# Attention and MoE on one core: the sign bit of a decoded weight from a multiplication by zero on GpSimd instead of a mask on VectorE

## The chip, the cores and the metric

The kernel runs on 1 core of one Trainium2 chip. The metric is the device time of one execution in microseconds (us). In the rows below PE is TensorE (PEld its weight loads), DVE is VectorE, ACT is ScalarE, POOL is GpSimd and SP is SyncE, which issues the DMAs.

## What is computed

The reference is attention that keeps the 32 best scores of each row, followed by four matrix products:

```python
scores = (q @ k.transpose(0, 1, 3, 2)) / sqrt(64)      # batch 8, heads 8, 576 x 576, head size 64
kth = np.partition(scores, -32, axis=-1)[..., -32:-31]
scores = np.where(scores >= kth, scores, -1e9)
attn = exp(scores - max); attn = attn / (sum(attn) + 1e-9)
x = (attn @ v) laid out as 4608 tokens x 512
out = (((x @ w1) * (x @ w2)) @ w3) @ w_out             # 512 -> 1024 -> 1024 -> 512
```

q, k and v are float32, the weights float64: each weight reaches the chip as a pair of 32-bit words, a low word and a high word, and the kernel turns the pair into a float32 by itself.

## The kernel before

**Attention slots.** The work is cut into 144 slots (8 batches, 18 slots each; a slot is 128 queries of two heads). The loop of line 504 runs over `p` and is software-pipelined: in turn `p` VectorE looks for the 32 best of slot `p` (`top32_steps`), GpSimd and ScalarE mask and exponentiate slot `p-1` (`edges_of`, `mask`, `exps`), TensorE computes the scores of slot `p+1`, and slot `p-2` is transposed, multiplied with V and normalised. Below "slot n" means turn `p = n` of this loop, counted from the moment VectorE starts the four min/max operations at its head (`w<-s` twice, `w<-w,s` twice), which I call the opening. `mask` may only start after the opening of the same turn (line 509).

**MoE blocks.** Every 12 slots give 384 tokens; their matrix products (`moe_steps`) are put in between the slots by `fill`, 24 matmuls a turn. The first block needs slots 0 to 11 through to their normalisation, so it starts in turn 14.

**Weights at the start.** 80 units of 128 x 256 weights (16 of `w_out`, 32 of `w3` mixed with 16 of `w1`, then 16 of `w2`) are fetched and decoded in turns 0 to 13. `warm` (line 487) is called six times a turn; each call takes one new unit and moves every unit on the way by one step, oldest first. For a unit taken in call k the steps are:

- call k: ScalarE writes `t`, the high word scaled by 2^-112, into PSUM, and `r`, the upper 16 bits of the low word scaled by 2^-13, as an integer into SBUF (lines 115, 116). Two units share a PSUM tile for `t`.
- call k+1: VectorE cuts the sign bit out of `t` (line 119, the **sign cut**), then shifts `t` left by 3 and ors the sign in (line 120, the **shift-or**), giving `u`.
- call k+2: GpSimd adds `u` and `r` as integers (line 123, the **integer add**).
- call k+4 and later: a `w3` unit is multiplied with `w_out` on TensorE (`pf`), because `w3 @ w_out` is folded into one matrix; every fourth one ends with a cast to `wf` on ScalarE and a subtraction on VectorE. A `w1` or `w2` unit is cast to `wh` on ScalarE and, one call later, its rest `wl` is computed by GpSimd (`wl<-z,wh`).

All engines run what they are given in program order (`InOrder`, line 47), so an instruction that waits holds up everything behind it on its engine. In the trace every operation carries the line of that helper, L57; rows are told apart by their tiles.

The line of the change reads, before:

```python
sign, u, r = (z[:, i * 256 : (i + 1) * 256].bitcast(I32) for i in range(3))
...
dve.tensor_scalar(sign, ti, -(2**31), None, op0=ALU.bitwise_and)
dve.scalar_tensor_tensor(u, ti, 3, sign, op0=ALU.logical_shift_left, op1=ALU.bitwise_or)
```

`z` has 768 words; the pairs fill 0 to 511. So `sign` and `u` were written over the pairs once ScalarE had read them, and `r` behind them.

Of the kernel before, what the change touches and what calls it, by code (L numbers as in the profile page):

```python
# [11 lines left out]
I32 = mybir.dt.int32  # L12
U16 = mybir.dt.uint16
AF = mybir.ActivationFunctionType
ALU = mybir.AluOpType
# [52 lines left out]
def attn_moe(ctx: ExitStack, tc: tile.TileContext, q, k, v, w1, w2, w3, w_out, out, flag, general):  # L68
    nc = tc.nc
    pe, act, dve, pool, sp = nc.tensor, nc.scalar, nc.vector, nc.gpsimd, nc.sync  # L70
# [26 lines left out]
    if not general:  # L97
        pe, act, dve, pool, sp = (InOrder(tc, e) for e in (pe, act, dve, pool, sp))
# [8 lines left out]
    def decode(z, dst=None):  # L107
        if not bank:
            both = ps_m.tile([128, 512], F32, tag="mm", name="t")
            bank.extend((both[:, 256:], both[:, :256]))  # L110
        t = bank.pop()
        high = z[:, 1:512:2]
        low = z[:, :512].bitcast(U16)[:, 1:1024:4]
        sign, u, r = (z[:, i * 256 : (i + 1) * 256].bitcast(I32) for i in range(3))
        act.activation(t, high, AF.Copy, scale=2.0**-112)
        act.activation(r, low, AF.Copy, scale=2.0**-13)
        yield
        ti = t.bitcast(I32)
        dve.tensor_scalar(sign, ti, -(2**31), None, op0=ALU.bitwise_and)
        dve.scalar_tensor_tensor(u, ti, 3, sign, op0=ALU.logical_shift_left, op1=ALU.bitwise_or)  # L120
        yield
        dst = z[:, :256] if dst is None else dst
        pool.tensor_tensor(dst.bitcast(I32), u, r, op=ALU.add)
        yield
        yield
        return dst

    def load_w12(i, c, z):
        if len(wl) == i:
            wl.append(const.tile([128, NCC * DF], F32R, tag="wl1", name="wl1"))  # L130
        cut = slice(c * 256, (c + 1) * 256)
        y = yield from decode(z)
        act.copy(wh[i][:, cut], y)
        yield
        pool.tensor_tensor(wl[i][:, cut], y, wh[i][:, cut].bitcast(F32), op=ALU.subtract)

    def load_wout(c, z):
        yield from decode(z, wo[:, c * 256 : (c + 1) * 256])
# [3 lines left out]
    def load_w3(c, z):  # L142
        f, i = c // 4, c % 4
        y = yield from decode(z)
        if i == 0:
            fold[f] = ps_m.tile([128, 512], F32, tag="mm", name=f"pf{f}")
        for j in range(2 * i, 2 * i + 2):
            pe.matmul(
                fold[f], y[:, (j % 2) * 128 : (j % 2 + 1) * 128], wo[:, j * DM : (j + 1) * DM],
                start=(j == 0), stop=(j == NFC - 1),  # L150
            )
        if i == 3:
            cut = slice(f * DM, (f + 1) * DM)
            yield
            act.copy(wf[0][:, cut], fold[f])
            yield
            dve.tensor_tensor(wf[1][:, cut], fold[f], wf[0][:, cut].bitcast(F32), op=ALU.subtract)
# [273 lines left out]
    for n in range(n_blocks):  # L431
        mine = sorted({group_of[i] for i in range(n * BLOCK, (n + 1) * BLOCK)}, key=lambda g: groups[g])
        lo, pieces = 0, []
        for g in mine:
            b, t = groups[g]
# [68 lines left out]
    for p in range(-1, n_slots + 3):  # L504
        i, j, m = p + 1, p - 1, p - 2
# [29 lines left out]
        if i < n_slots:  # L535
            b, hps, t = slots[i]
# [10 lines left out]
        if 0 <= m < n_slots:  # L547
            b, hps, t = slots[m]
# [86 lines left out]
```

## Time and profile before

| | |
|---|---|
| median of 3 runs | 1319.36 us (1319.17 to 1322.74) |
| the profiled execution | 1321.85 us, span 1320.0 us |
| TensorE busy | 1235.3 us, 94% of the span |
| VectorE busy | 1194.1 us, 90% |
| ScalarE busy | 965.9 us, 73% |
| GpSimd busy | 853.7 us, 65% |
| weights decoded | from 7.2 us (first `t`) to 207.0 us (last `wl`) |

How to read it: the profiled execution lies 2.49 us above the median, and its span 1.85 us below its own time. The shares are averages over two very different stretches, turns 0 to 13 with the decoding and the turns after them, so a view by stretch is needed.

### The profile page before, as it was taken

The page shows a single profiled execution, that of the slowest core. Times are in us where ns is not written, and L with a number is a line of the kernel's source. Part 1 is how long each engine was busy: PE and PEld are TensorE (multiplying, and loading weights), DVE is VectorE, ACT ScalarE, POOL GpSimd, SP SyncE. Part 2 cuts the span into 40 slices and gives each one's busy share as a digit, 9 for nine tenths or more (in the row PEclk, how much of TensorE's full clock was granted, in tenths as well). Part 3 has the DMA queues.
Part 4 walks back from the last instruction along what each step waited for, and adds up shares of the span by engine and source line. Part 5 has one row for each costly group of instructions (what it writes and reads, how often), then busy time and mean ns, then how long its engine had stood idle before and what let it go on. Part 6 is the DMA issues. An engine that isn't in the chain of part 4 may idle for free.

```text
span 1320.0 us, 28196 instructions
## 1 busy us (share of the span) xinstructions
PE 1235.3 (94%) x9617; PEld 1047.7 (79%) x9617; DVE 1194.1 (90%) x4012; ACT 965.9 (73%) x2057; POOL 853.7 (65%) x1225
## 2 busy tenths in 40 slices
PE   2788858999999999999999999999999999999996
PEld 1334436888888888888888888888888888888996
DVE  7988898999999999999999999999999999999610
ACT  5766786877777877777877877778777778777621
POOL 4767697666766766667757757757667666667510
PEclk9899967999999999999999999999999999999998
DMA  6333331200121001100120012110220012000000
GB/s 243 91 101 123 110 96 29 81 22 21 29 74 32 9 27 64 53 27 16 39 84 20 10 33 79 32 33 10 65 60 9 15 47 81 22 21 1 13 13 27
DMA packets 35886, 64.82 MB, mean 49 GB/s; under 512 B 6036, under 2 KB 12180, under 8 KB 35732
## 3 DMA queue, kind: packets, MB, share of 16 engines
q1 hardware_dynamic: 35732, 62.93, 15.3%
q8 instruction: 77, 1.26, 0.4%
q14 instruction: 77, 0.63, 0.2%
HBM read 53.48 MB, written 9.44 MB: 48 GB/s over the span
## 4 chain that ended last, share of the span: by engine, by line
PE 87%; DVE 4%; POOL 3%; ACT 2%; issue 2%; DMA 1%; SPq 0%; POOLq 0%
PE ab L57 32%; PE eo L57 16%; PE ro L57 15%; PE st L57 12%; PE tp L57 9%; PE pf L57 3%; DVE z L57 2%; DVE w L57 1%; POOL z L57 1%; DVE top L57 1%; POOL wl L57 1%; ACT pab L57 1%; DMA vt<-in_v 0%; ACT s L57 0%; ACT z L57 0%
## 5 line engine op out<-in xcount | busy, mean ns | idle before, releaser
L57 POOL TENSOR_TENSOR pab<-s,pab 128x576 f32<-128x576 f32 x288 | 404.2, 1426 | 127.5 <-DVE w L57 102.0
L57 DVE MAX8 top<-w 128x8 f32<-128x192 f32 (+1 forms) x1152 | 467.3, 447 | 0.0
L57 PE MATMUL ab<-x,wh 128*128 128x384 f32 x1536 | 403.7, 344 | 0.0
L57 ACT COPY pts<-tp 128x1024 f32<-128x1024 f32 x144 | 146.1, 1014 | 198.2 <-PE tp L57 196.8
L57 DVE MATCH_REPLACE8 w<-top,w 128x192 f32<-128x192 f32 x864 | 289.4, 343 | 0.0
L57 PEld LDWEIGHTS ab<-x,wh 128*128 128x128 f32 x1536 | 275.3, 189 | 0.0
L57 PE MATMUL ab<-x,wl 128*128 128x384 f32 x768 | 269.5, 351 | 0.0
L57 ACT ACTIVATE pab<-pab,edge 128x576 f32<-128x576 f32 x288 | 226.8, 787 | 0.5 <-POOL pab L57 0.5
L57 PE MATMUL eo<-g,wf 128*128 128x384 f32 x1152 | 225.8, 346 | 0.0
L57 ACT ACTIVATE pab<-s,edge 128x576 f32<-128x576 f32 x288 | 207.6, 768 | 7.6 <-POOL edge L57 7.5
L57 PE MATMUL st<-kt,qt 64*128 64x288 f32 (+1 forms) x1280 | 188.7, 443 | 18.4 <-ACT pts L57 7.4
L57 PEld LDWEIGHTS eo<-g,wf 128*128 128x128 f32 x1152 | 198.6, 188 | 7.5 <-issue 7.5
L57 ACT COPY s<-st 128x576 f32<-128x576 f32 x288 | 184.4, 640 | 19.5 <-PE st L57 19.5
L57 DVE TENSOR_TENSOR w<-w,s 128x384 f32<-128x384 f32 x288 | 183.9, 639 | 4.9
L57 DVE TENSOR_TENSOR w<-s 128x384 f32<-128x384 f32 x288 | 173.0, 642 | 7.4 <-ACT s L57 7.4
L57 PEld LDWEIGHTS ro<-pts,vt 128*64 128x64 f32 x2560 | 130.2, 139 | 51.3 <-ACT g L57 28.3
L57 PEld LDWEIGHTS st<-kt,qt 64*128 64x128 f32 (+1 forms) x1280 | 100.6, 183 | 81.0 <-ACT pr L57 28.1
L57 PE MATMUL ro<-pts,vt 128*64 128x128 f32 (+1 forms) x2560 | 163.4, 271 | 0.0
L57 PE MATMUL tp<-ident,pab 128*128 128x128 f32 x1152 | 152.1, 275 | 11.3 <-ACT s L57 11.3
L57 PEld LDWEIGHTS ab<-x,wl 128*128 128x128 f32 x768 | 144.3, 188 | 13.4 <-issue 12.3
L57 PEld LDWEIGHTS tp<-ident,pab 128*128 128x128 f32 x1152 | 136.4, 142 | 22.3 <-POOL wo L57 10.7
L57 POOL TENSOR_TENSOR g<-asb,g 128x384 fp32r<-128x384 f32 x96 | 96.9, 1010 | 86.8 <-ACT g L57 86.8
(51 smaller groups left out, 1309.6 us busy)
## 6 DMA issues: line engine op xcount, KB each, us to landing
z<-in_w SPq DMA_DIRECT2D x64, 256.0 KB, 2.7
vt<-in_v SPq DMA_DIRECT2D x32, 352.0 KB, 3.7
qt<-in_q SPq DMA_DIRECT2D x40, 256.0 KB, 2.7
kt<-in_k SPq DMA_DIRECT2D x32, 320.0 KB, 3.1
out_t<-osb SPq DMA_DIRECT2D x32, 192.0 KB, 1.9
z<-in_wo SPq DMA_DIRECT2D x16, 256.0 KB, 3.9
out_t<-osb SPq DMA_DIRECT2D x16, 160.0 KB, 1.8
out_t<-osb SPq DMA_DIRECT2D x16, 32.0 KB, 1.6
```

Of the source, the lines that this page charges most:

```text
L57: ins = fn(*args, **kw)
```

## The change

The sign bit is no longer cut out of `t` by VectorE. GpSimd multiplies the high words by 0.0, which leaves a zero with the sign of the weight, and writes it to words 512 to 767 of the tile (I call it the **zero product**). The shift-or takes it from there and writes `u` over it. `r` now goes into the low words of the pairs, with a stride of two words, and the integer add writes its sum over `u` unless the unit is one of `w_out`.

```diff
-        sign, u, r = (z[:, i * 256 : (i + 1) * 256].bitcast(I32) for i in range(3))
+        r, u = z[:, 0:512:2].bitcast(I32), z[:, 512:768].bitcast(I32)
         act.activation(t, high, AF.Copy, scale=2.0**-112)
+        pool.tensor_scalar(z[:, 512:768], high, 0.0, None, op0=ALU.mult)
         act.activation(r, low, AF.Copy, scale=2.0**-13)
         yield
-        ti = t.bitcast(I32)
-        dve.tensor_scalar(sign, ti, -(2**31), None, op0=ALU.bitwise_and)
-        dve.scalar_tensor_tensor(u, ti, 3, sign, op0=ALU.logical_shift_left, op1=ALU.bitwise_or)
+        dve.scalar_tensor_tensor(u, t.bitcast(I32), 3, u, op0=ALU.logical_shift_left, op1=ALU.bitwise_or)
         yield
-        dst = z[:, :256] if dst is None else dst
+        dst = z[:, 512:768] if dst is None else dst
         pool.tensor_tensor(dst.bitcast(I32), u, r, op=ALU.add)
```

GpSimd's order in a turn with `w3` and `w1` units, from `sums` (head of the turn) on. `edge`, `over`, `x` and `wide` belong to the attention, `pab` is the attention masking, `z<-z` as TENSOR_TENSOR the integer add. Before:

```order
L57 TENSOR_SCALAR sums<-sums 128x2
L57 TENSOR_TENSOR z<-z 128x256
L57 TENSOR_TENSOR edge<-top_96,coef 128x4
L57 TENSOR_TENSOR over<-top_96 128x2
L57 TENSOR_TENSOR x<-pr,x 128x128
L57 COPY wide<-sums 128x128
L57 TENSOR_TENSOR pab<-s,pab 128x576 x2
L57 TENSOR_TENSOR wl_103<-z,wh_98 128x256
L57 TENSOR_TENSOR z<-z 128x256
L57 TENSOR_TENSOR wl_103<-z,wh_98 128x256
L57 TENSOR_TENSOR z<-z 128x256 x4
```

The same stretch in the changed kernel (`TENSOR_SCALAR z<-z` is the zero product):

```order
L57 TENSOR_SCALAR sums<-sums 128x2
L57 TENSOR_TENSOR z<-z 128x256
L57 TENSOR_SCALAR z<-z 128x256
L57 TENSOR_TENSOR edge<-top_96,coef 128x4
L57 TENSOR_TENSOR over<-top_96 128x2
L57 TENSOR_TENSOR x<-pr,x 128x128
L57 COPY wide<-sums 128x128
L57 TENSOR_TENSOR pab<-s,pab 128x576 x2
L57 TENSOR_TENSOR wl_103<-z,wh_98 128x256
L57 TENSOR_TENSOR z<-z 128x256
L57 TENSOR_SCALAR z<-z 128x256
L57 TENSOR_TENSOR wl_103<-z,wh_98 128x256
```

One zero product stands ahead of `edge`, the other five of the turn stand behind the masking, each behind the integer add of its call and ahead of the next call's work.

VectorE's order in such a turn with what each row waits for, from the `wf` subtraction on. Before:

```order
L57 TENSOR_TENSOR wf_101<-pf_734,wf_100 128x512 [waits Activation_49]
L57 TENSOR_SCALAR z<-t 128x256 [waits DMAHW7_49,Activation_49]
L57 SCALAR_TENSOR_TENSOR z<-t,z 128x256 [waits DVE_49]
L57 MAX top_95<-w 128x8 x2
L57 MATCH_REPLACE w<-top_95,w 128x192 [waits DVE_49] x2
L57 TENSOR_SCALAR z<-t 128x256 [waits DMAHW0_49,Activation_49]
```

In the changed kernel:

```order
L57 TENSOR_TENSOR wf_101<-pf_868,wf_100 128x512 [waits Activation_49]
L57 SCALAR_TENSOR_TENSOR z<-t,z 128x256 [waits DMAHW4_49,Activation_49,Pool_49]
L57 MAX top_96<-w 128x8 x2
L57 MATCH_REPLACE w<-top_96,w 128x192 [waits DVE_49] x2
L57 SCALAR_TENSOR_TENSOR z<-t,z 128x256 [waits DMAHW6_49,Activation_49,Pool_49]
```

The sign cuts are gone, and the shift-or now waits for GpSimd as well.

## Rows read from the trace of the kernel before

**Rows 1.** The first part of the page: busy time, share of the span and instructions of each engine.

```profile
PE 1235.3 (94%) x9617; PEld 1047.7 (79%) x9617; DVE 1194.1 (90%) x4012; ACT 965.9 (73%) x2057; POOL 853.7 (65%) x1225
```

**Rows 2.** Busy time by stretch, one stretch a turn: slots 0, 1, 2, then 5 and 6, then 11, 12, 13, and last the time from slot 14 to 1290 us. Columns: stretch, its length, then busy us (and instructions) of PE, PEld, DVE, ACT and POOL, the granted TensorE clock, the DMA engines' busy share, GB/s.

```profile
7.38:18.19 10.81, 4.58 (x16) 2.45 (x16) 10.60 (x35) 4.49 (x12) 2.91 (x4) 1.00 1.04 390
18.19:30.54 12.35, 2.15 (x9) 1.78 (x9) 12.04 (x38) 8.24 (x20) 8.37 (x11) 1.00 0.46 131
30.54:43.39 12.85, 7.15 (x38) 4.36 (x38) 12.33 (x40) 9.73 (x23) 8.66 (x12) 1.00 0.46 146
...
72.87:89.07 16.20, 12.97 (x56) 6.23 (x55) 13.30 (x41) 10.81 (x26) 10.71 (x15) 0.89 0.35 99
89.07:103.64 14.57, 11.33 (x56) 5.75 (x55) 13.31 (x42) 10.83 (x26) 10.74 (x15) 1.00 0.42 127
...
165.15:179.63 14.48, 9.49 (x52) 6.03 (x50) 13.29 (x41) 12.25 (x31) 12.82 (x19) 0.76 0.41 110
179.63:194.09 14.46, 7.84 (x38) 4.88 (x38) 13.27 (x40) 11.52 (x30) 13.53 (x20) 0.54 0.37 109
194.09:206.35 12.26, 6.67 (x38) 4.29 (x38) 10.81 (x34) 9.24 (x23) 12.11 (x18) 0.56 0.01 1
206.35:1290.00 1083.65, 1080.68 (x8896) 957.27 (x8897) 1014.72 (x3479) 820.07 (x1707) 709.18 (x1016) 1.00 0.12 36
```

**Rows 3.** VectorE's groups by shape, the two of the decoding: count, then busy us and mean ns of one, then idle time before them and what ended it.

```profile
L57 DVE SCALAR_TENSOR_TENSOR z<-t,z 128x256 int32<-128x256 int32 x80 | 34.0, 424 | 2.7
L57 DVE TENSOR_SCALAR z<-t 128x256 int32<-128x256 int32 x80 | 33.3, 417 | 8.1 <-ACT z L57 7.6 <-issue 0.4
```

**Rows 4.** VectorE in order of time in slot 1: start us, duration us. Two units follow each other here without anything between them.

```profile
20.72 0.42 DVE L57 TENSOR_SCALAR z<-t 128x256 int32<-128x256 int32 x1
21.17 0.42 DVE L57 SCALAR_TENSOR_TENSOR z<-t,z 128x256 int32<-128x256 int32 x1
21.51 0.41 DVE L57 TENSOR_SCALAR z<-t 128x256 int32<-128x256 int32 x1
```

**Rows 5.** GpSimd's groups by shape that bear on the price of the zero product (columns as in rows 3).

```profile
L57 POOL TENSOR_SCALAR sums<-sums 128x2 f32<-128x2 f32 x144 | 30.9, 214 | 119.6 <-ACT pab L57 118.6 <-DVE top L57 0.5
L57 POOL TENSOR_TENSOR wl<-z,wh 128x256 fp32r<-128x256 f32 x32 | 23.3, 729 | 1.3 <-ACT wh L57 1.0
...
L89 POOL MEMSET over<- 128x288 f32 x1 | 0.3, 338 | 0.0
...
masks.py:197 POOL MEMSET ident<- 128x128 f32 x1 | 0.2, 205 | 0.3 <-POOLq L618 0.3
```

**Rows 6.** Order of time in slot 1: the integer add at the turn's head, the masking, and the third shift-or of the turn.

```profile
18.41 0.92 POOL L57 TENSOR_TENSOR wo<-z 128x256 int32<-128x256 int32 x1 [1.38 <-issue]
...
20.95 2.77 POOL L57 TENSOR_TENSOR pab<-s,pab 128x576 f32<-128x576 f32 x2 [0.68 <-DVE w L57]
...
23.92 0.42 DVE L57 SCALAR_TENSOR_TENSOR z<-t,z 128x256 int32<-128x256 int32 x1
```

**Rows 7.** Order of time in slot 6, all engines (start us, duration us; in brackets the idle time of the engine before it and what ended it).

```profile
90.93 0.59 ACT L57 CAST wf<-pf 128x512 fp32r<-128x512 f32 x1 [1.03 <-PE pf L57]
...
92.37 1.43 ACT L57 ACTIVATE pab<-s,edge 128x576 f32<-128x576 f32 x2
...
93.22 2.78 POOL L57 TENSOR_TENSOR pab<-s,pab 128x576 f32<-128x576 f32 x2 [1.10 <-ACT pab L57]
...
95.97 0.72 POOL L57 TENSOR_TENSOR wl<-z,wh 128x256 fp32r<-128x256 f32 x1
...
96.65 0.72 POOL L57 TENSOR_TENSOR z<-z 128x256 int32<-128x256 int32 x1
...
97.42 1.98 PE L57 MATMUL pf<-wo,z 128*128 128x512 f32 x4 [2.63 <-POOL z L57]
...
98.00 0.42 DVE L57 SCALAR_TENSOR_TENSOR z<-t,z 128x256 int32<-128x256 int32 x1
...
99.34 1.24 PE L57 MATMUL st<-kt,qt 64*128 64x288 f32 x8
...
100.14 0.64 ACT L57 COPY s<-st 128x576 f32<-128x576 f32 x1 [0.92 <-PE st L57]
...
100.51 1.09 PE L57 MATMUL ro<-pts,vt 128*64 128x128 f32 x16
...
101.75 2.41 PE L57 MATMUL pf<-wo,z 128*128 128x512 f32 x5
101.94 0.29 DVE L57 TENSOR_TENSOR pr<-ro,pr 128x128 f32<-128x128 f32 x1 [0.22 <-POOL sums L57]
...
102.77 0.42 DVE L57 TENSOR_SCALAR z<-t 128x256 int32<-128x256 int32 x1 [0.54 <-ACT z L57]
...
103.64 0.54 DVE L57 TENSOR_TENSOR w<-s 128x384 f32<-128x384 f32 x1
```

**Rows 8.** GpSimd in order of time in slots 11 and 12: the first instruction behind the masking of slot 11, the two rows of these slots behind the masking that had idle time before them, and the `sums` that ends slot 11.

```profile
172.02 0.73 POOL L57 TENSOR_TENSOR wl<-z,wh 128x256 fp32r<-128x256 f32 x1
...
177.81 0.73 POOL L57 TENSOR_TENSOR wl<-z,wh 128x256 fp32r<-128x256 f32 x1 [0.25 <-ACT wh L57]
...
179.30 0.21 POOL L57 TENSOR_SCALAR sums<-sums 128x2 f32<-128x2 f32 x1
...
192.26 0.73 POOL L57 TENSOR_TENSOR wl<-z,wh 128x256 fp32r<-128x256 f32 x1 [0.76 <-ACT wh L57]
```

## The prediction

> **What bounds the kernel now.** I read the page first: TensorE is busy for 94% of the span and VectorE for 90% [rows 1]. Such shares hide that the change touches only the first sixth of the run, so the second view is busy time by turn. From slot 14 to 1290 us TensorE is busy for 1080.68 of 1083.65 us [rows 2]: that stretch is bound by TensorE, nothing is decoded in it, and the change does not reach it. The work that TensorE does there cannot start before turn 14, so a microsecond won or lost in turns 0 to 13 is won or lost in the total. In these turns TensorE is not full, and the limit changes: in slots 0 and 1 VectorE is busy for 10.60 of 10.81 and 12.04 of 12.35 us; in slot 6 it is busy for 13.31 of 14.57; in slots 11 to 13 GpSimd comes up, 13.53 of 14.46 and 12.11 of 12.26 us [rows 2]. So there are three stretches with three limits, and I cost the change in each.
>
> **What goes and what comes.** VectorE loses 80 sign cuts of 417 ns [rows 3]. Started back to back, a sign cut takes 0.45 us of its queue and a shift-or 0.34 [rows 4], so 0.45 us a unit, 2.7 us in a turn of six units, 36 us in all. GpSimd gains 80 zero products. The trace has none of that size. The nearest row is the same operation on 128x2, 214 ns; the two MEMSETs, 338 ns for 288 elements and 205 for 128, differ by 133 ns for 160 elements, 0.83 ns an element [rows 5]. 214 ns and 254 elements more come to 425 ns. GpSimd starts the next instruction some 0.04 us before the last ends (the 0.72 us subtraction at 95.97 is followed at 96.65 [rows 7]), so I take **c = 0.40 us** of its queue. The lower end is a pure write, 0.30 us (the MEMSET of 288); the upper end the two-input subtraction on 128x256, 729 ns, so 0.69 us [rows 5]. I stay near the low end because the product reads one operand, like the TENSOR_SCALAR row. The Trainium skill's page "GPSIMD Engine Reference" speaks against the change in its section "Engine selection": element-wise work belongs on VectorE, GpSimd is about twice as slow with two inputs, roughly at line rate with one. By its two-input ratio a product would cost about 0.8 us and the sum below would end near +10 us; by its one-input remark it stays where it is. The MEMSETs' 0.83 ns an element agree with the remark; no row here shows a one-input operation of this size. The integer add, the shift-or and ScalarE's two operations keep their element counts and, I assume, their times.
>
> **Slot 0: a gain of 2.0 us.** Nothing is masked yet, VectorE is the limit, and GpSimd has 7.9 us to spare of 10.81 [rows 2]. Five sign cuts go, 5 x 0.45 = 2.25 us. The DMA engines are busy throughout (share 1.04), bringing in the later units, so I keep 2.0.
>
> **Slots 1 to 3: the gain turns into a new wait.** The shift-or of the unit taken behind the masking must now wait for its zero product, which stands behind the masking in GpSimd's queue. In slot 1 the masking starts at 20.95 and takes 2.77 [rows 6]. At the head of the turn the opening and GpSimd's work hold each other up (the integer add takes 0.92 us there [rows 6]), so the product put ahead of `edge` delays the masking by its own 0.40 and about 0.25 of one more turn-taking: 21.6. Masking 2.73, integer add 0.69, product 0.40 and 0.1 for the semaphore bring the third shift-or to 25.5, where it starts at 23.92 now [rows 6]. From it to the next opening there are now 30.54 - 23.92 = 6.62 us [rows 2, 6]; three sign cuts fewer make it 5.27, so the opening comes at 30.8 instead of 30.54: 0.25 later, relative to the start of the slot. The same sum gives -0.1 for slot 2. VectorE's 2.7 us a turn are spent on waiting for GpSimd. In slot 3 the first weight product on TensorE starts behind `wide`, which moves back by about 0.45 us. Slots 0 to 3 together hand on -2.0 + 0.25 - 0.1 + 0.45 = **-1.4 us**.
>
> **Slots 4 to 10: nothing.** The chain that repeats here does not contain the sign cut. In slot 6 it runs: cast `wf` 90.93 (after 1.03 us of waiting for TensorE), ScalarE's row to the relu 92.37, masking 93.22 (waited 1.10 for ScalarE), `wl` 95.97, integer add 96.65, weight product `pf` 97.42 (waited 2.63 for GpSimd), scores 99.34, values 100.51, `pf` again 101.75, whose end lets the next cast start [rows 7]. Every link starts where the one before ends, once around is the slot, and no zero product stands between the masking and the integer add that `pf` waits for. VectorE has its own chain beside it. Its fourth shift-or, at 98.00 now, must wait for masking end 95.97, two `wl`, two adds and two products: 95.97 + 4 x 0.69 + 2 x 0.40 + 0.1 = 99.6. From there to the opening it took 5.64 us, with two sign cuts and two waits (0.22 and 0.54) in it [rows 7]; without them 3.98, so the opening comes at 103.6, where it is now (103.64). ScalarE writes the next `t` after that shift-or and is late by up to 1.6 us; 0.92 of it was idle ahead of the score copies at 100.14, and 1.03 ahead of the cast [rows 7]. So the freed VectorE time becomes waiting, and the turn keeps its length. Slot 5, with the same work at a clock of 0.89, has 16.20 instead of 14.57 us [rows 2]: there the cover is wider still.
>
> **Slots 11 to 13: a loss of 4.2 us.** No weight product runs here any more, but every call has an integer add and a `wl` on GpSimd. Behind the masking of slot 11 GpSimd works from 172.02 to the `sums` at 179.30 with only 0.25 us of idle time; in slot 12 it has 0.76 [rows 8]. Each waits for a cast on ScalarE that the products give time for. Slot 11 takes five products behind the masking, slot 12 six, slot 13 the last two: 5 x 0.40 - 0.25 + 6 x 0.40 - 0.76 + 2 x 0.40 = **+4.2 us**. VectorE does not shorten these turns: the reciprocal ahead of its opening waits for `sums`, in GpSimd's order.
>
> **The sum.** -1.4 + 0 + 4.2 = +2.8 us. The profiled execution took 1321.85 us, so the same one would be 1324.65; it stands 2.49 above the median, which gives **1322.2 us** beside 1319.36. In c the sum is 18 c - 4.4: 13 products in the last stretch, two places each in slots 1 and 2, one in slot 3. At c = 0.30 it is +1.0, at 0.69 +8.0, and there the opening in slots 4 to 10 slips as well, by some 0.5 us in the four turns at full clock, +10 in all.
>
> **Rivals.** *The loss in slots 11 to 13 is larger* (slower). It decides from c = 0.47 on, where 18 c - 4.4 passes 4.0 us, 0.3% of the median and about what a measurement of this kernel can tell from no change. For it: stride-two reads of GpSimd and a multiplication have no row of this size. Against it: the TENSOR_SCALAR and MEMSET rows. With c of 0.5 to 0.69 it ends at 1324 to 1329.5 us; chance 0.28.
>
> *The new wait reaches ScalarE* (slower): the shift-or holds back the next `t`, ScalarE's queue behind it the score copies, and these the cast `wf`, in slots 4 to 10. It decides where the shift-or slips by more than the 0.92 and 1.03 us that ScalarE has idle; each 0.3 us beyond costs 2 us in seven turns, so 1324 to 1326 us; chance 0.12. For it speaks that the copies stand right behind that `t`.
>
> *VectorE does pace slots 4 to 10* (faster). It is busy for 13.31 of 14.57 us in slot 6 [rows 2], and the sign cut at 102.77 stands close ahead of the opening. If the opening and not TensorE's chain set the turn, each would lose 0.6 to 1.0 us, seven turns 4 to 7, and with -1.4 and +4.2 the run ends at 1315 to 1318. Against it: all the links of rows 7 touch. Chance 0.10 for more than 0.3%.
>
> *The change does not do what it says*: `r` is written between the words that the product reads, and if ScalarE had to wait for the product, its queue would stand. ScalarE's order shows no such wait, so I give it 0.02, at 1335.
>
> **How the numbers follow.** Likeliest: 1322.2, inside 0.3% (1315.4 to 1323.3) with a chance of 0.48; the two slower rivals and the last give 0.42, the faster one 0.10. A whole turn more or fewer at the lower clock, 16.20 against 14.57 us, moves any case by 1.6. For 8 in 10 the range takes in c from 0.30 to 0.69 with little beyond, and the milder half of the faster rival: 1317.5 to 1329.5.
>
> **What would show it.** Right: slot 0 about 2 us shorter, VectorE idle ahead of the third and fourth shift-or with GpSimd named as releaser, slots 4 to 10 of the old lengths, slots 11 to 13 together about 4 us longer, the stretch from slot 14 on unchanged, and a zero product of 0.40 to 0.43 us. Wrong: a product above 0.5 us, or turns of slots 4 to 10 that get shorter with the links of rows 7 still closed, which would mean that I have misread the chain.

## The result, and the profile after

| | before | after |
|---|---|---|
| median | 1319.28 us (4 runs, 1319.17 to 1322.74) | 1337.62 us (4 runs, 1335.60 to 1338.73) |
| ratio | | 1.0131, 95% interval 1.0110 to 1.0152 |
| the profiled execution | 1321.85 us, span 1320.0 | 1335.60 us, span 1334.1 |

The changed kernel is slower by 1.3%, about 18 us between the medians and 13.75 us between the profiled executions (the one of after is its fastest, the one of before lies 2.6 us above its median). The forecast was 1322.2 us with a range to 1329.5, so it was wrong by 15.4 us, and the size of the loss lies outside of its range. Beside the experiments the kernel before had medians of 1321.4 to 1322.5 us, so each ratio below is against the runs of before made with it; set beside those medians, after's 1337.62 is a loss of 15 to 16 us.

The page of after, first part, against [rows 1]:

```profile
PE 1234.5 (93%) x9617; PEld 1047.0 (78%) x9617; DVE 1162.4 (87%) x3932; ACT 965.3 (72%) x2057; POOL 917.8 (69%) x1305
```

VectorE lost 31.7 us of work and GpSimd gained 64.1. Where that counts is seen by turn; columns as in [rows 2], here for slots 0, 1, 2, then 6 and 7, then 11, 12, 13 of after, and the time from slot 14 to 1290 us:

```profile
7.64:16.38 8.74, 4.24 (x16) 2.44 (x16) 8.57 (x30) 4.60 (x12) 5.04 (x7) 1.00 1.04 399
16.38:31.88 15.50, 2.50 (x11) 1.78 (x9) 10.10 (x33) 9.35 (x24) 14.60 (x20) 1.00 0.45 151
31.88:45.94 14.06, 7.12 (x38) 4.21 (x38) 10.14 (x34) 9.47 (x24) 13.72 (x19) 0.93 0.44 131
...
92.26:108.47 16.21, 12.71 (x60) 6.36 (x59) 10.85 (x34) 10.63 (x26) 15.52 (x22) 1.00 0.42 125
108.47:124.12 15.65, 12.68 (x56) 5.99 (x55) 10.87 (x35) 10.87 (x26) 15.49 (x22) 0.89 0.32 102
...
171.63:189.28 17.65, 7.80 (x47) 5.25 (x45) 10.93 (x34) 13.06 (x33) 17.51 (x25) 0.75 0.32 97
189.28:207.60 18.32, 7.84 (x38) 4.89 (x38) 10.86 (x33) 11.46 (x29) 18.18 (x26) 0.50 0.24 73
207.60:221.19 13.59, 6.80 (x38) 4.40 (x38) 9.58 (x30) 7.44 (x17) 13.41 (x19) 0.62 0.00 1
221.19:1290.00 1068.81, 1065.74 (x8817) 942.62 (x8817) 1012.89 (x3476) 817.04 (x1702) 704.91 (x1012) 1.00 0.11 36
```

Read the POOL column (the fifth pair) against each turn's length: 14.60 of 15.50, 15.49 of 15.65, 18.18 of 18.32. GpSimd is now full in nearly all turns; before, it had about 4 us to spare in slots 1, 2 and 6 and less only from slot 11 on [rows 2]. The loss is complete when slot 14 starts: at 221.19 us instead of 206.35, 14.84 later. From there to the end of the span both take the same, 1112.9 and 1113.7 us.

GpSimd's groups by shape in the first 225 us (columns as in [rows 5]) give the price of what was added:

```profile
L57 POOL TENSOR_SCALAR z<-z 128x256 f32<-128x256 f32 x80 | 74.3, 930 | 4.8 <-DMA z<-in_wo 4.8
L57 POOL TENSOR_TENSOR z<-z 128x256 int32<-128x256 int32 x64 | 48.3, 754 | 0.7
L57 POOL TENSOR_TENSOR wl<-z,wh 128x256 fp32r<-128x256 f32 x32 | 23.7, 743 | 0.8 <-ACT wh L57 0.6
```

A zero product takes 930 ns in the mean, more than the subtraction `wl` with its two inputs, which I had made the upper end. All 80 take 74.3 us, although GpSimd's busy time grew by only 64.1: 14 of them stand at the head of a turn, beside the opening, and take 1.16 to 1.19 us there, and small rows behind them get shorter (`over` 238 ns in the mean where it had 475, `wide` 312 for 571, both in the first 225 us). And this is slot 6 of after, to be read against [rows 7]:

```profile
96.23 2.77 POOL L57 TENSOR_TENSOR pab<-s,pab 128x576 f32<-128x576 f32 x2 [0.53 <-ACT pab L57]
...
98.96 0.72 POOL L57 TENSOR_TENSOR wl<-z,wh 128x256 fp32r<-128x256 f32 x1
...
99.64 0.73 POOL L57 TENSOR_TENSOR z<-z 128x256 int32<-128x256 int32 x1
...
100.34 0.86 POOL L57 TENSOR_SCALAR z<-z 128x256 f32<-128x256 f32 x1
...
100.43 1.98 PE L57 MATMUL pf<-wo,z 128*128 128x512 f32 x4 [2.62 <-POOL z L57]
...
101.17 0.73 POOL L57 TENSOR_TENSOR wl<-z,wh 128x256 fp32r<-128x256 f32 x1
101.24 0.42 DVE L57 SCALAR_TENSOR_TENSOR z<-t,z 128x256 int32<-128x256 int32 x1 [3.65 <-POOL z L57]
...
103.93 0.41 ACT L57 ACTIVATE t<-z 128x256 f32<-128x256 f32 x1 [3.58 <-DVE z L57]
...
108.39 0.17 DVE L57 RECIPROCAL sums<-sums 128x2 f32<-128x2 f32 x1 [1.05 <-POOL sums L57]
```

From 100.34 to 101.17 a product holds GpSimd's queue for c = 0.83 us. The shift-or behind it waits 3.65 us, ScalarE's next `t` 3.58, and at the turn's end the reciprocal ahead of VectorE's next opening waits for `sums`, which is the last in GpSimd's order: that wait is what ties the turn to the length of GpSimd's work.

### The profile page after: what moved, and what is told of

Same layout as the page of the kernel before. It is cut to its first block, busy times and chain, and to the rows that moved or that the text cites. A ratio compares the mean times of both kernels' runs of the same rounds, so it can differ in the third digit from the quotient of the medians.

```text
span 1334.1 us, 28138 instructions
## 1 busy us (share of the span) xinstructions
PE 1234.5 (93%) x9617; PEld 1047.0 (78%) x9617; DVE 1162.4 (87%) x3932; ACT 965.3 (72%) x2057; POOL 917.8 (69%) x1305
## 4 chain that ended last, share of the span: by engine, by line
PE 86%; POOL 7%; ACT 3%; issue 1%; DVE 1%; DMA 0%; POOLq 0%; SPq 0%; DVEq 0%; ACTq 0%
PE ab L57 32%; PE eo L57 16%; PE ro L57 15%; PE st L57 12%; PE tp L57 9%; POOL z L57 4%; PE pf L57 2%; POOL wl L57 1%; POOL pab L57 1%; ACT pab L57 1%; DVE w L57 1%; ACT t L57 1%; ACT z L57 1%; DVE z L57 0%; POOL wo L57 0%
## 5 line engine op out<-in xcount | busy, mean ns | idle before, releaser
L57 DVE TENSOR_TENSOR w<-w,s 128x384 f32<-128x384 f32 x288 | 181.2, 629 | 4.9
L57 DVE TENSOR_TENSOR w<-s 128x384 f32<-128x384 f32 x288 | 175.9, 651 | 7.6 <-ACT s L57 7.6
```

The costliest lines, as they stand in the source:

```text
L57: ins = fn(*args, **kw)
```

## The experiments

Two readings fit the trace of after. **Theory A:** the time of the products in GpSimd's queue makes the loss, and the waits of VectorE and ScalarE only show it. **Theory B:** the new wait of the shift-or, passed on to ScalarE, makes the loss of slots 1 to 10. The table gives, for the profiled execution of each kernel, the lengths of the groups of turns in us, and the start of slot 14.

| kernel | slot 0 | 1 to 3 | 4 to 10 | 11 to 13 | slot 14 at |
|---|---|---|---|---|---|
| before | 10.81 | 38.59 | 108.36 | 41.21 | 206.35 |
| after | 8.74 | 43.84 | 111.41 | 49.56 | 221.19 |
| e1_cut_only | 10.79 | 38.31 | 110.97 | 41.12 | 208.64 |
| e2_cut_and_product | 10.79 | 42.44 | 110.97 | 49.60 | 221.22 |
| e3_neither | 10.28 | 33.64 | 117.93 | 41.15 | 210.46 |
| e5_copy | 9.23 | 38.14 | 119.91 | 45.58 | 220.43 |
| e6_slot0 | 9.51 | 38.15 | 108.55 | 40.94 | 204.74 |
| e7_slot0_act | 8.89 | 36.44 | 109.45 | 41.27 | 203.43 |
| e8_to_slot10 | 9.35 | 43.77 | 110.59 | 40.44 | 211.64 |
| e9_mask_zero | 10.80 | 37.40 | 113.45 | 41.15 | 210.36 |
| e10_cut_and_copy | 10.79 | 38.75 | 108.62 | 45.01 | 210.62 |
| e11_two_inputs | 8.95 | 42.21 | 109.83 | 49.75 | 218.16 |

In all of them the time from slot 14 to the end of the span is 1112.1 to 1114.4 us, so the last column carries the comparison. Each row is one execution, and the executions of one kernel lie 2 to 12 us apart, the longer ones mostly at a lower mean granted clock of TensorE; so 2 or 3 us between two rows in slots 4 to 10 show nothing by themselves.

**e1_cut_only: the layout alone.** The edits are against the changed kernel, here and below.

```diff
-        pool.tensor_scalar(z[:, 512:768], high, 0.0, None, op0=ALU.mult)
+        dve.tensor_scalar(u, t.bitcast(I32), -(2**31), None, op0=ALU.bitwise_and)
```

> The changed kernel's layout (r with a stride of two words, the shift-or writing into words 512 to 767), but the sign cut back on VectorE and no zero product. Theory A (the loss is GpSimd's time in the zero products) and theory B (the loss is the new wait of the shift-or for GpSimd) both expect the time of before, 1319 us within 4 us, slot 0 at 10.8 us, the strided r on ScalarE at about 0.42 us and the integer add at about 0.75. If the layout costs something by itself, the time would lie above 1323 us and these two durations above those.

Measured: 1320.11 us against 1322.52, ratio 0.9983 (0.9973 to 0.9992). The strided `r` (0.43 us, before 0.42) and the other place of `u` (the integer add 0.78, before 0.77) cost nothing; if anything they gain 2 us. That the table has slot 14 later by 2.3 us is no contradiction: the profiled execution, 1322.47 us, is one of the longest of the ten, with slot 8 at 17.27 us and a granted clock of 0.80.

**e2_cut_and_product: GpSimd's work alone.** The sign cut as in e1, and the product into columns that hold only zeros yet.

```diff
+        pool.tensor_scalar(over[:, 32:288], high, 0.0, None, op0=ALU.mult)
...
+        dve.tensor_scalar(u, t.bitcast(I32), -(2**31), None, op0=ALU.bitwise_and)
```

> Sign cut on VectorE as in e1_cut_only, and the zero product as well, written to a place that nobody of the decoding reads: GpSimd's work of the change without the wait of the shift-or and without VectorE's relief. Theory A (GpSimd's queue, 80 products of 0.83 us in it, makes the loss; the wait is only where it shows): 1333 to 1341 us, slots 11 to 13 together 8 us longer than before, slots 1 to 3 about 4 to 6, slots 4 to 10 about 3. Theory B (the new wait of the shift-or passes on to ScalarE's next t and makes the loss of slots 1 to 10): only slots 11 to 13 get longer, about 1327 us.

Measured: 1335.58 us, ratio 1.0104 (1.0087 to 1.0121). Three of its turns (slots 1, 8, 12):

```profile
18.21:32.37 14.16, 2.16 (x9) 1.78 (x9) 12.28 (x39) 9.62 (x24) 13.34 (x18) 1.00 0.39 117
...
124.67:140.31 15.64, 12.53 (x56) 6.01 (x55) 13.21 (x40) 10.97 (x26) 15.48 (x22) 0.89 0.34 105
...
189.29:207.63 18.34, 7.15 (x38) 4.47 (x38) 13.22 (x40) 11.62 (x29) 18.18 (x26) 0.59 0.25 73
```

Nobody waits for these products, VectorE has all its sign cuts, and yet slots 8 and 12 take 15.64 and 18.34 us as in after and slot 14 starts within 0.03 us of after's. Theory A stands. Theory B falls as the account of the loss: it expected 1327 us. Slot 1 alone is longer in after, 15.50 us, and that is not the wait either. Slot 0 of after is 2.05 us shorter, so the end of an integer add and one whole product come over from it, ahead of the masking. In after and here the masking starts at

```profile
21.05 2.77 POOL L57 TENSOR_TENSOR pab<-s,pab 128x576 f32<-128x576 f32 x2 [0.74 <-ACT pab L57]
```

```profile
21.54 2.77 POOL L57 TENSOR_TENSOR pab<-s,pab 128x576 f32<-128x576 f32 x2 [0.42 <-ACT pab L57]
```

which is 4.67 and 3.33 us behind the turn's head (16.38 and 18.21), all of the difference; GpSimd is busy for 14.60 of 15.50 us and for 13.34 of 14.16. So most of what VectorE wins in slot 0 goes back to GpSimd's queue in slot 1. By the times alone a small cost of the wait is not excluded: the ratios 1.0104 and after's 1.0131 have intervals that overlap.

**e3_neither: VectorE's relief alone.** The weights lose their sign.

```diff
-        pool.tensor_scalar(z[:, 512:768], high, 0.0, None, op0=ALU.mult)
...
-        dve.scalar_tensor_tensor(u, t.bitcast(I32), 3, u, op0=ALU.logical_shift_left, op1=ALU.bitwise_or)
+        dve.tensor_scalar(u, t.bitcast(I32), 3, None, op0=ALU.logical_shift_left)
```

> Neither sign cut nor zero product: VectorE only shifts, so the weights lose their sign; what is left is VectorE's relief alone. If VectorE paces only slots 0 to 3, the gain is about 2 us in slot 0 and 1.4 to 2.7 in each of slots 1 and 2, none in slots 4 to 10 (the chain TensorE, ScalarE, GpSimd) and none in 11 to 13: 1313 to 1315 us. If VectorE paces slots 4 to 10 as well, each of these gets 0.6 us or more shorter and the time is 1309 us or less.

Measured: 1323.83 us (1313.64 to 1326.12), ratio 0.9998 (0.9979 to 1.0016): the median meets neither expectation. The shortest of the ten runs, 1313.64 us at a mean granted clock of 0.978, lies in the first; the profiled one, 1325.10, had 0.968. In its table row slots 0 to 3 are 5.5 us shorter than before, and slots 4 to 10 are 9.6 longer: two of these took 16.20 and 15.94 us at 0.89, about what before has at that clock (16.09 to 16.21), and five took 17.07 to 17.23 at 0.80. Slot 7 of e3_neither as a turn, and ScalarE and TensorE in its slot 6:

```profile
100.75:117.96 17.21, 13.48 (x55) 6.68 (x54) 10.94 (x35) 10.67 (x27) 10.58 (x15) 0.80 0.31 93
```

```profile
86.45 0.59 ACT L57 CAST wf<-pf 128x512 fp32r<-128x512 f32 x1 [2.12 <-PE pf L57]
...
87.35 1.88 PE L57 MATMUL pf<-wo,z 128*128 128x512 f32 x4
92.95 3.78 PE L57 MATMUL pf<-wo,z 128*128 128x512 f32 x4 [3.73 <-POOL z L57]
96.67 2.11 PE L57 MATMUL st<-kt,qt 64*128 64x288 f32 x8
```

In [rows 7] the same four matmuls take 1.98 us and the scores 1.24, after a wait of 2.63. Two more rows of before, the four matmuls ahead in slot 6 and the ones behind the wait in slot 7:

```profile
92.81 1.98 PE L57 MATMUL pf<-wo,z 128*128 128x512 f32 x4 [0.31 <-DVE z L57]
...
111.99 3.19 PE L57 MATMUL pf<-wo,z 128*128 128x512 f32 x4 [2.62 <-POOL z L57]
```

Here TensorE starts the four matmuls ahead of them 0.9 us after the `wf` cast (87.35 against 86.45) instead of 1.9 (92.81 against 90.93 before), waits 3.73 us for the integer add, which hangs on the masking as before, and then runs at the lower of its two clocks: 3.78 us for the four with a granted clock of 0.50 (1.2 GHz), 0.80 in the mean of the turn. Before has the lower clock behind this wait too, in slots 4, 5, 7 and 9 and for part of the time, though the wait is 2.6 us in each of its turns; so the length of the wait alone does not say when the clock falls. A lighter VectorE, in any case, did not shorten these turns.

**e9_mask_zero: is it the wrong weights?** Against e1_cut_only:

```diff
-        dve.tensor_scalar(u, t.bitcast(I32), -(2**31), None, op0=ALU.bitwise_and)
+        dve.tensor_scalar(u, t.bitcast(I32), 0, None, op0=ALU.bitwise_and)
```

> e1_cut_only with a mask of 0 in place of the sign's: the same instructions with the same times on every engine, but the weights lose their sign as in e3_neither. It asks why slots 4 to 10 of e3_neither and e5_copy took 17.1 us each at a granted TensorE clock of 0.80. If the wrong weights do it, this kernel shows the same 17.1 us turns and a time of 1327 us or more. If it is the order of events (a lighter VectorE leaves TensorE a longer gap ahead of the weight product), slots 4 to 10 are those of e1_cut_only, mostly 14.8 to 16.0 us, and the time is that of e1_cut_only, 1317 to 1323 us.

Measured: 1323.02 us (1317.48 to 1324.75), ratio 1.0002 (0.9987 to 1.0017). Three of its seven turns took 17.3 us at 0.80, the others 14.8 to 16.0; in e1_cut_only it was one. TensorE's waits ahead of those weight products, 2.9 to 3.5 us, are those of e1_cut_only and not the 3.7 of e3_neither. So the weights may add turns at the lower clock, but with e1_cut_only's order of events they do not bring the five and seven in a row that e3_neither and, below, e5_copy have. Whether right weights would show such a row with a light VectorE was not run: in after and e11_two_inputs, where they are right, GpSimd paces most of these turns. In which turn the clock falls stays open, since a wait of 3.24 us was followed by 3.78 us for the four matmuls in slot 5 and a wait of 3.26 by 1.98 in slot 6.

**e4_prices: what the operation costs by itself.** Added behind all other work, four times each:

```diff
+            pool.tensor_scalar(o, src[:, 1:512:2], 0.0, None, op0=ALU.mult)   # mul_even
+            pool.tensor_scalar(o, src[:, :256], 0.0, None, op0=ALU.mult)      # mul_flat; mul_half: 128 columns
+            pool.tensor_scalar(o, src[:, :256], 0.0, None, op0=ALU.add)       # add_flat
+            pool.tensor_copy(o, src[:, 1:512:2])                              # copy_even; copy_flat: [:, :256]
+            pool.tensor_tensor(o, src[:, :256], src[:, 512:], op=ALU.mult)    # two_flat
```

> The changed kernel, with seven operations of GpSimd on 128x256 f32 (one on 128x128) added at its end, four times each. If the price of the zero product comes from its operation (about 2.6 ns an element, (880 - 214) / 254), mul_flat costs 0.86 to 0.88 us like mul_even, mul_half 0.54, add_flat 0.87. If it comes from reading every second word, mul_flat costs about 0.43 us, mul_half 0.3 and copy_even twice copy_flat. The product of two tensors (two_flat) should cost 0.73 us as the subtraction of wl does. The total is some 15 to 25 us above the changed kernel's, at the very end.

GpSimd's groups by shape from 1290 us to the end (1351.44 us in all, one run; 13.8 above after's median, where 15 to 25 were expected):

```profile
L57 POOL TENSOR_SCALAR mul_even<-src 128x256 f32<-128x256 f32 x4 | 3.5, 864 | 0.3
L57 POOL TENSOR_SCALAR add_flat<-src 128x256 f32<-128x256 f32 x4 | 3.4, 854 | 0.2
L57 POOL TENSOR_SCALAR mul_flat<-src 128x256 f32<-128x256 f32 x4 | 3.4, 848 | 0.2
L57 POOL TENSOR_TENSOR two_flat<-src 128x256 f32<-128x256 f32 x4 | 2.9, 722 | 0.2
L57 POOL TENSOR_SCALAR mul_half<-src 128x128 f32<-128x128 f32 x4 | 2.1, 528 | 0.2
L57 POOL COPY copy_even<-src 128x256 f32<-128x256 f32 x4 | 1.6, 405 | 0.2
L57 POOL COPY copy_flat<-src 128x256 f32<-128x256 f32 x4 | 1.6, 400 | 0.2
```

The price belongs to the operation: 848 ns without a stride, 864 with one. An add costs what a multiplication does, and (848 - 528) / 128 = 2.5 ns an element is three times the slope of the MEMSETs. The copy costs the 0.40 us that I had put down for the product, and the product of two tensors is cheaper than that of a tensor and a constant.

**e5_copy: the forecast's price, in the same place.**

```diff
-        pool.tensor_scalar(z[:, 512:768], high, 0.0, None, op0=ALU.mult)
+        pool.tensor_copy(z[:, 512:768], high)
```

> The changed kernel with a COPY of the high words on GpSimd in place of their product with zero: same place, same operands, same wait of the shift-or, but 0.40 us instead of 0.86 (e4_prices). The shift-or then ors the whole high word in, so the weights keep their sign and get sizes between 1 and 2. It asks whether the forecast failed by the price alone. Theory A (price): the forecast's sum with c = 0.44, the queue step of a copy in e4_prices, gives 18 x 0.44 - 4.4 = +3.5 us, and slots 4 to 10 fall back to TensorE's chain, so 3 to 5 us above the kernel before on the same chip, 1323 to 1327 us. Theory B (the wait as such is what costs): slots 1 to 10 stay as long as in the changed kernel and only part of slots 11 to 13 comes back, 1330 us or more.

Measured: 1332.47 us, ratio 1.0062 (1.0039 to 1.0085), four runs of 1325.84, 1332.33, 1332.62 and 1334.60 us with mean granted clocks of 0.975, 0.967, 0.967 and 0.962. The first lies in theory A's 1323 to 1327, the others by their time in theory B's, and slot by slot the profiled one (1334.60) says why. Slots 1, 7 and 12:

```profile
16.80:30.01 13.21, 1.96 (x9) 1.78 (x9) 10.06 (x33) 8.24 (x20) 11.56 (x19) 1.00 0.55 180
...
106.39:123.55 17.16, 13.44 (x55) 6.68 (x54) 10.99 (x36) 10.71 (x27) 12.85 (x21) 0.80 0.31 93
...
191.72:207.48 15.76, 7.81 (x38) 4.89 (x38) 10.87 (x33) 11.24 (x30) 15.61 (x26) 0.50 0.33 96
```

By the table slots 0 to 3 are 2.0 us shorter than before, and slots 11 to 13 are 4.4 longer; the forecast had -1.4 and +4.2. Slots 1 to 3 came back by 5.7 us from after's length although the wait is still there, against theory B. But slots 4 to 10 take 11.6 us more than before, all seven at 0.80 like five of e3_neither: no longer paced by GpSimd (12.85 of 17.16 us), with a light VectorE, they run into the same lower clock. The weights differ here too, so by this run alone their part is not told apart.

**e10_cut_and_copy: the same price with right weights and VectorE as before.** Against e2_cut_and_product:

```diff
-        pool.tensor_scalar(over[:, 32:288], high, 0.0, None, op0=ALU.mult)
+        pool.tensor_copy(over[:, 32:288], high)
```

> e2_cut_and_product with a COPY in place of the unread product: weights right, VectorE as before, 0.44 us more on GpSimd's queue for each unit instead of 0.83. Theory A (the price decides): slots 11 to 13 together 13 x 0.44 - 1.01 = 4.7 us longer than before, slots 4 to 10 on TensorE's chain as before since GpSimd is then busy for 12.9 of 14.6 to 16.2 us, slots 1 to 3 at most 1.5 longer: 4 to 6 us above the kernel before on the same chip. Rival: any GpSimd work in slots 4 to 10 delays the integer add and with it the weight product, then these turns are longer by 0.4 us each or lose the clock (17.1 us turns), 8 us or more above.

Measured: 1326.43 us against 1322.21, ratio 1.0035 (1.0020 to 1.0049), 4.2 us above as theory A expected. Slots 8 and 12:

```profile
120.26:134.84 14.58, 11.25 (x55) 5.73 (x54) 13.27 (x41) 10.74 (x26) 12.86 (x21) 1.00 0.35 108
...
181.90:197.66 15.76, 6.96 (x38) 4.17 (x38) 13.20 (x39) 11.52 (x29) 15.59 (x26) 0.61 0.32 96
```

Slots 4 to 10 take 108.62 us (before 108.36), slots 11 to 13 3.8 us more than before, where 4.7 were expected: between the kernel's own instructions a copy holds the queue for 0.37 us (174.13 to 174.50 in slot 11) and not for e4_prices' 0.44, and 13 x 0.37 - 1.01 is 3.8.

**e8_to_slot10: no products in slots 11 to 13.**

```diff
+        k = next(units)
+        if k < 65:
             pool.tensor_scalar(z[:, 512:768], high, 0.0, None, op0=ALU.mult)
...
+        if not (k < 65):
+            dve.tensor_scalar(u, t.bitcast(I32), -(2**31), None, op0=ALU.bitwise_and)
```

> The zero product for the 65 units of turns 0 to 10, the sign cut on VectorE for the last 15. If slots 11 to 13 cost what GpSimd's queue says there, they come back to 14.5, 14.5 and 12.3 us and the time is 8.4 us below the changed kernel's, 1327 to 1330 us. If VectorE's sign cuts had been the limit there, or if the loss is carried in from earlier turns, less than half of that comes back: 1333 us or more.

Measured: 1327.01 us, ratio 1.0040 (1.0024 to 1.0055), 10.6 us below after's median. The last three turns come back to 40.44 us (before 41.21), 9.1 us less than in after; the products of those turns cost that much (slot 12 is back at 14.11 us with GpSimd busy for 13.57).

**e11_two_inputs: a cheaper product.** The same columns of zeros as in e2, read this time:

```diff
-        pool.tensor_scalar(z[:, 512:768], high, 0.0, None, op0=ALU.mult)
+        pool.tensor_tensor(z[:, 512:768], high, over[:, 32:288], op=ALU.mult)
```

> The changed kernel with the zero product made from two tensors (the high words times 256 columns that still hold zeros) in place of a tensor and a constant: by e4_prices 0.72 us instead of 0.85, so 0.13 us less on GpSimd's queue for each of 80 units, and everything else alike. If GpSimd's queue sets the loss, slots 11 to 13 give back 13 x 0.13 = 1.7 us and slots 1 to 3 up to 0.8 each; in slots 4 to 10 GpSimd is busy for 14.7 instead of 15.5 us, so these fall back to TensorE's chain, 14.6 to 16.2. Together 3 to 8 us below the changed kernel, 1329 to 1334 us. Rival: with GpSimd no longer pacing, slots 4 to 10 go into the 17.1 us turns at a granted clock of 0.80 that e3_neither and e5_copy show; then no gain over the changed kernel, or a loss.

Measured: 1334.12 us, ratio 1.0107 (1.0090 to 1.0124), 3.5 us below after's median, and in the table slot 14 starts 3.0 us earlier: slots 1 to 3 give back 1.6 us and slots 4 to 10 1.6, but slots 11 to 13 nothing, against an expected 1.7. Slot 12 does give back 0.5 us, but slot 11 takes 18.34 us instead of 17.65: GpSimd is busy for 17.04 of it, half a microsecond less, and now waits 1.08 us for ScalarE ahead of the masking, which in slot 11 of after it does not:

```profile
168.41:186.75 18.34, 10.58 (x53) 6.45 (x51) 11.22 (x34) 13.49 (x35) 17.04 (x25) 0.68 0.32 96
```

```profile
173.21 2.76 POOL L57 TENSOR_TENSOR pab<-s,pab 128x576 f32<-128x576 f32 x2 [1.08 <-ACT pab L57]
```

Why ScalarE comes later there was not followed up. In slots 4 to 10 GpSimd is busy for 15.0 us a turn, not the 14.7 expected, so slots 4, 5, 7 and 10 (15.13 to 15.43 us) are still paced by it or nearly so; the other three take 16.2 to 16.4.

**e6_slot0: products only where GpSimd is idle.** As e8_to_slot10, with `k < 6`.

> The zero product for the first six units alone (turn 0, where GpSimd is idle for most of the time), the sign cut on VectorE for the other 74. Slot 0 should be 2.0 us shorter as in the changed kernel, slot 1 by one sign cut, 0.4, and all else as before: 1.5 to 2.5 us below the kernel before (ratio 0.998 to 0.999). Rival, after e3_neither: what is won ahead of slot 4 is given back there in turns at a lower granted clock of TensorE (17.1 us at 0.80 against 14.6 at 1.00), so no gain or a small loss.

Measured: 1318.55 us (9 runs, 1317.86 to 1319.80) against 1321.68, ratio 0.9977 (0.9967 to 0.9987). It is below both kernels, by 0.2% below before. Slot 0 is 1.3 us shorter, where 2.0 were expected, slot 1 0.35. But e1_cut_only, without any product, had 0.9983 (0.9973 to 0.9992): how much of the gain is the products' is not told apart.

**e7_slot0_act: six more signs from ScalarE.** As e6_slot0, and for units 7, 9, 11, 13, 15 and 17 in place of the cut:

```diff
+            act.activation(z[:, 512:768], high, AF.Copy, scale=0.0)
```

> As e6_slot0, and for every second unit of turns 1 and 2 (six in all) ScalarE makes the signed zero (a copy with scale 0, 0.42 us by the t rows). VectorE's turns 1 and 2 lose 1.35 us of sign cuts each, ScalarE has 12.35 - 8.24 and 12.85 - 9.73 us to spare there: 1.0 to 1.3 us shorter each, 4 to 5 us below the kernel before in all (ratio 0.9965). Rival: as for e6_slot0, given back in slots 4 to 10 at a lower granted clock; then no gain although slots 0 to 3 are 4 us shorter.

Measured: 1320.98 us, ratio 0.9994 (0.9983 to 1.0005). The weights are no longer all right: it looks as if ScalarE's copy with scale 0.0 leaves a zero without a sign, so that six units lose theirs, but no run looks at that zero by itself. Slots 0 to 3 are 4.1 us shorter than before, but slot 4 is one of the turns at 0.80:

```profile
52.71:69.84 17.13, 13.84 (x55) 6.59 (x54) 13.21 (x41) 10.83 (x26) 10.63 (x15) 0.80 0.31 92
```

In the profiled run slot 14 still starts 2.9 us earlier than before; by the medians no gain is left that can be told from none.

## Why the prediction was wrong

**The step that failed is the price c of the zero product.** I took 0.40 us of GpSimd's queue, with ends at 0.30 and 0.69; it is 0.83 in the stretches behind the masking. I worked it out from a TENSOR_SCALAR on two columns (214 ns) and the slope of the MEMSETs (0.83 ns an element) [rows 5], since the product reads one operand. e4_prices shows that slope to be 2.5 ns. The nearest row was the one that I had made the upper end: an arithmetic operation of the same size, `wl` with 729 ns [rows 5]; a MEMSET reads nothing. The slope of arithmetic was in the trace of before as well: a masking row on 576 elements takes 1.41 us in the mean of the first 225 us, `wl` on 256 takes 0.73, 2.1 ns an element, which with the 214 ns for two elements makes an estimate of about 750 ns. And the upper end was no bound: one tensor and a constant costs more than two tensors. The Trainium skill's page "GPSIMD Engine Reference", section "Engine selection", has about a factor of two against VectorE for two inputs and roughly line rate for one. The trace agrees with the factor in an operation that has one tensor input, 880 ns (median) against 417 for the sign cut of the same size on VectorE, 2.1; with the line rate only for COPY, 0.40 us. By that factor, which I set aside, the sum was +10 us.

**A second step failed beside it: the path of slots 1 and 4 to 10.** The forecast counted the products only where they stand in a chain that it had traced, and did not add all six to GpSimd's busy time of the turn. At 0.40 us that would have cost nothing (10.7 and 2.4 are 13.1 of 14.55 us); at 0.83 it is most of the rest of the loss.

Point by point, with what c = 0.83 makes of the terms:

- **Slot 0**, -2.0: right, -2.07 (its start is 0.26 later).
- **Slots 1 to 3**, +0.25, -0.1, +0.45: with the right c the same sums give +1.1, +0.8 and +0.9; measured +3.15, +1.21 and +0.89. Slot 1 is the one still far off. I counted the products in two places of the path; at 0.83 us all of GpSimd's queue is the path, with seven products in the turn (one came in from slot 0): 14.60 us busy instead of 8.37.
- **Slots 4 to 10**, nothing: +3.05. The mechanism that I named for them, masking, integer add, weight product, is still closed in slot 6 of after. But GpSimd's own work is 15.5 us a turn now, so the turns of 14.55 us cannot be had any more; e2_cut_and_product has the same floor without the wait. "Nothing" holds for a copy's price, 0.37 in the queue, if VectorE keeps its sign cuts (e10_cut_and_copy). It did not hold when VectorE lost them (e5_copy, where the weights differ too): there TensorE's wait is longer, 3.4 to 3.7 us instead of 2.6, and its clock falls behind it, neither of which I had seen.
- **Slots 11 to 13**, +4.2: the mechanism right, the size wrong by c. 13 x 0.83 - 1.01 = 9.8, measured 8.35; e8_to_slot10 takes it back, and at the copy's price it is +4.4 and +3.8 (e5_copy, e10_cut_and_copy; the sum with 0.37 gives 3.8).
- **The sum**, 18 c - 4.4: at 0.83 it gives +10.5, where slot 14 starts 14.84 us later. The missing 4.3 are slots 1, 2 and 4 to 10 (2.0, 0.4 and 3.05) and the later start of slot 0, less the 1.4 by which slots 11 to 13 fell short.
- **The rivals.** The larger loss in slots 11 to 13 came true, beyond its own price of 0.5 to 0.69. The wait does reach ScalarE (3.58 us ahead of `t`), but e2_cut_and_product shows the loss without it. VectorE pacing slots 4 to 10 finds no support in e3_neither, whose turns at 0.89 are as long as before's; a turn at 1.00 with so light a VectorE is in no trace. ScalarE does not wait for the product with `r`.

Shown by runs: the price, that GpSimd's queue and not the wait carries the loss, and that slots 11 to 13 hold the larger part of it. Argued from the traces only: that TensorE's longer wait is what brings the lower clock in e3_neither and e5_copy. A row of e11_two_inputs (slot 7) speaks against the wait as the whole reason, since the clock was at 0.50 behind a wait of 1.08 us as well:

```profile
113.06 3.78 PE L57 MATMUL pf<-wo,z 128*128 128x512 f32 x4 [1.08 <-POOL z L57]
```

Filling that wait without other changes was not tried.

## What to carry to other kernels

Before work is moved to another engine, add it to that engine's busy time turn by turn and compare with the length of the turn: 10.7 us and six products of 0.83 are 15.7 (measured 15.5), above the 14.55 us of the fast turns, and for that no chain has to be followed. Take a price from the row of the same kind of work (arithmetic on a tensor of that size), set the upper end above the dearest row that is like it, and where a factor of two in one price decides the sign, let the range hold it. Relief of an engine that does not set the turn was worth nothing here, and in two kernels it went with a lower clock of the engine that does.

## What the runs showed of the hardware

- GpSimd, 128x256 f32: COPY 0.40 us, product of two tensors 0.72, tensor and constant 0.85 (multiplication and addition alike); a stride of two words in the source adds 1 to 2% (e4_prices).
- Beside VectorE's opening a zero product takes longer (slot 6 of after):

```profile
92.26 1.80 DVE L57 TENSOR_TENSOR w<-s 128x384 f32<-128x384 f32 x2
...
92.93 1.19 POOL L57 TENSOR_SCALAR z<-z 128x256 f32<-128x256 f32 x1
```

  1.19 us instead of 0.86. The two operations of VectorE take 1.80 us, in e1_cut_only's slot 6 1.55, but the whole opening takes 2.82 us in both (92.26 to 95.08, and 88.67 to 91.49): other rows of GpSimd run beside it there.
- In slots 4 to 10, where GpSimd does not pace the turn (before, e1_cut_only, e3_neither, e5_copy, e10_cut_and_copy), a turn takes about 14.6 to 14.9, 16 or 17.2 us at mean granted clocks of 1.00, 0.89 and 0.80. Whole runs of one kernel differ along with their mean clock: e5_copy had 1325.84 us at 0.975 and 1334.60 at 0.962; of these only the second has a trace.
